# A causal attention kernel with a token sort woven into it: the order of two PSUM readers, of ScalarE's copy, of scatters and loads, and a padded tail

## The chip, the cores and the metric

The kernel runs on one core of one Trainium2 chip. The metric is the device time of one execution in microseconds; lower is better. The runs below fell on three chips, called chip 1, chip 5 and chip 15. A kernel is compared with the kernel before in rounds on the same chip only. Every run here counts as fast but one timed run of the kernel before on chip 15 (881.96 us); the ratios leave it out, the median of 872.19 us has it in. The record does not say on which chip the first comparison ran, nor on which the kernel before was profiled.

## The reference

Attention with a decaying bias is followed by a mixture of experts in which a token goes through one of 8 experts, its own choice or that of the token before it.

```python
batch, n_heads, seq, head_dim = (8, 8, 576, 64)          # experts: 8, D 512, F 1024
scores = q @ k.T / sqrt(64)
cum = cumsum(max(s, 0)); bias = -(cum[i] - cum[j])
scores = where(causal, -1e9, scores + min(bias, 0))
attn = softmax(scores); x = attn @ v                     # -> (8, 576, 512)
logits = x @ w_gate; local_gate = sigmoid(x @ w_local)
for b, s in tokens:                                      # in order of s
    fresh_e = argmax(logits[b, s])
    e = fresh_e if s == 0 or local_gate[b, s] < 0.5 else prev_e
    prev_e = e
    out[b, s] = softmax(logits[b, s])[e] * (relu(x[b, s] @ w1[e]) @ w2[e])
```

## The kernel before

Attention goes through 32 pairs of heads, four pairs to a batch. Scores are held transposed (keys on the partitions), so the sums over keys are TensorE products with a column of ones. 576 is 4 blocks of 128 and a tail of 64. While TensorE makes the scores of pair n, it also finishes pair n - 1: values, sums, and the turning back of x to rows. One iteration:

```python
for n in range(NPAIR + 1):
    b, hp = divmod(n, HP)
    ...                                # loads of q, k, for the next batch
    if b + 1 < B and hp == 1:          # (in the kernel, nested)
        load_v(b + 1, slice(0, HP))    # four transfers of 256 KB at once
    if n + 2 < NPAIR: load_tail(n + 2) # four transfers of 16 KB
    if n: add_up(n - 1)                # VectorE: partial sums of exponentials
    for u, pieces in enumerate((((0, 0), (3, 1)), ((0, 1), (1, 1)), ((2, 0), (2, 1)))):
        scores(n, u)                   # TensorE
        weights(n, *pieces)            # ScalarE: two exponentials a piece; GpSimd: select on the diagonal
    for f in plan.pop((n, 0), ()): f(bank)      # sort work, place 0
    values(n - 1, 0); values(n - 1, 1)          # TensorE; xT copied by VectorE (0) and ScalarE (1)
    weights(n, (1, 0))
    for f in plan.pop((n, 1), ()): f(bank)      # sort work, place 1
    sums(n - 1)      # 36 one-column and 2 two-column products (the trace has two entries for each), then VectorE's reciprocal "recs"
    back(n - 1)      # TensorE: x in rows, VectorE multiplies by recs
    tail(n + 1)
    for f in plan.pop((n, 2), ()): f(bank)      # sort work, place 2
```

The tokens of a group of batches are sorted by expert as soon as its attention is done, in small steps put into the pairs that follow. The groups of batches 0-1, 2-3, 4 and 5 meet their codes in pairs 10, 18, 22 and 26. Their rows go to DRAM by indirect scatters from GpSimd, five to a batch:

```python
for bs in ((0, 1), (2, 3), (4,), (5,)):
    n = HP * bs[-1] + HP + 1
    ...
    at(n + 1, 1, g.fresh, g.share)
    ...
    for i, f in enumerate(g.scatters):
        i = 11 + i // 2 * 2            # two at each second place
        at(n + i // 3, i % 3, f)

def fresh(self, bank):                 # reads the transposed codes in PSUM, 2 x 576
    ...
    nc.scalar.activation(v[:, a:z], x, Act.Relu, bias=...)              # r_v
    nc.vector.tensor_scalar(u[:, a:z], x, 0.0, None, Alu.is_equal)      # r_u

def scatter(self, b, t):
    nc.gpsimd.indirect_dma_start(out=rows_in_dram, out_offset=slots, in_=self.xs[b][:z, t, :], ...)
```

After attention come the experts, about 565 us of dense products.

Of the kernel before, what the change touches and what calls it, by code (L numbers as in the profile page):

```python
# [18 lines left out]
P = 128  # L19
# [44 lines left out]
@with_exitstack  # L64
def kernel(
    ctx: ExitStack,
    tc: tile.TileContext,
    q: bass.AP,
    k: bass.AP,
    vm: bass.AP,  # L70
    vt: bass.AP,
    s: bass.AP,
    w_gate: bass.AP,
    w_local: bass.AP,
    w1: bass.AP,
    w2: bass.AP,
    out: bass.AP,
):
    nc = tc.nc
    mm, tr = nc.tensor.matmul, nc.tensor.transpose  # L80
    cum_d = nc.dram_tensor("cum", (B * H, S), F32, kind="Internal")
    x_d = nc.dram_tensor("x_tokens", (N, D), F32, kind="Internal")
    rows_d = nc.dram_tensor("x_rows", (E * R + 2 * P, XW), F32, kind="Internal")

    ctx.enter_context(tc.manual_schedule(engines=None))
    const = ctx.enter_context(tc.tile_pool(name="const", bufs=1))
    ident = const.tile([P, P], F32, name="ident")
    make_identity(nc, ident)
    lg = const.tile([P, NM, E + 1], F32, name="lg")
    nc.vector.memset(lg, 0.0)  # L90
    recs = const.tile([P, NPAIR, 2 * NB], F32, name="recs")
    nc.vector.memset(recs, 1.0)
    out_of = const.tile([P, 2], I32, name="out_of")
    sort = Sort(tc, const, lg, rows_d, ident)

    with ExitStack() as main:
        keep = main.enter_context(tc.tile_pool(name="keep", bufs=1))
        x4 = keep.tile([P, 4 * NB * XW], F32, name="x4")
        xs = {}

        def new_x(b):
            xs[b] = x4[:, b % 4 * NB * XW : (b % 4 + 1) * NB * XW].rearrange("p (t w) -> p t w", w=XW)
            return xs[b]


        plan = {}

        def at(n, half, *what):
            plan.setdefault((n, half), []).extend(what)

        for bs in ((0, 1), (2, 3), (4,), (5,)):
            n = HP * bs[-1] + HP + 1
            g = sort.group(bs, xs)
            at(n, 1, g.choose)
            at(n, 2, g.codes)
            at(n + 1, 0, g.rows)
            at(n + 1, 1, g.fresh, g.share)
            at(n + 1, 2, g.held)
            at(n + 2, 0, g.hold)
            at(n + 2, 1, g.hot, g.gates)  # L120
            at(n + 3, 0, g.count)
            at(n + 3, 1, g.rank)
            for i, f in enumerate(g.scatters):
                i = 11 + i // 2 * 2
                at(n + i // 3, i % 3, f)
        at(3, 1, sort.constants)
        at(26, 2, sort.early)
        gx = main.enter_context(tc.tile_pool(name="gx", bufs=5))
        w = keep.tile([P, WS], F32, name="w0")
        ready = {"w": {0: w}, "x": {}}  # L130
        for i in range(8):
            at(16 + i // 2, i % 2 * 2, lambda bank, i=i: load_weights(nc, w, w1, w2, EARLY[0], (i,)))

        def fetch_early(bank):
            for i, e in enumerate(EARLY):
                for k in range(2):
                    ready["x"][i, k] = gx.tile([P, XW], F32, name="xg")
                    r0 = e * R + k * P
                    nc.sync.dma_start(ready["x"][i, k], rows_d[r0 : r0 + P, :])

        at(28, 1, fetch_early)

        fx = main.enter_context(tc.tile_pool(name="fx", bufs=2))
        turned = ready["turned"] = Turned(nc, fx, main.enter_context(tc.tile_pool(name="first", bufs=2)), ident)
        for i in range(2):
            at(30 + i, 0, lambda bank, i=i: turned.product(0, i, 2, ready["x"][0, i], bank(1)[0]))
            at(30 + i, 1, lambda bank, i=i: turned.copies(0, i, ready["x"].pop((0, i))))
        last = sort.group((6, 7), xs)

        attention(tc, q, k, vm, vt, s, w_gate, w_local, ident, lg, recs, const, new_x, plan)  # L150
        tables = sort.tables()
        check = in_range(main.enter_context(tc.tile_pool(name="g_sb", bufs=1)), nc, recs, sort.total, sort.ones, out_of)
        hooks = [(2, last.choose), (2, last.codes), (6, last.rows), (6, last.fresh), (6, last.held), (8, last.share),
                 (11, last.hold), (11, last.hot), (13, last.count), (13, last.rank), (15, last.gates),
                 (16, lambda bank: [f(bank) for f in last.scatters]),
                 *((18 + 2 * i, lambda bank: next(tables, None)) for i in range(8)),
                 *((60 + 6 * i, lambda bank, f=f: f(bank)) for i, f in enumerate(check))]
        experts(tc, w1, w2, out, rows_d, ident, sort, early_units() + units(), hooks, x4[:, :WS], gx, ready)
    def number(x, most):
        return nc.values_load(x[0:1, 0:1], min_val=0, max_val=most, skip_runtime_bounds_check_because="a count")  # L160

    ALL = P * NPAIR * 2 * NB
    with tc.If(number(out_of[:, 1:], ALL + MOST[2]) > 0):
        total = number(sort.total, MOST[2])
        with tc.If(total > SLOTS[2]):
            experts(tc, w1, w2, out, rows_d, ident, sort, units(SLOTS[2], SLOTS[2] + 4))
            with tc.If(total > SLOTS[2] + 4):
                experts(tc, w1, w2, out, rows_d, ident, sort, units(SLOTS[2] + 4, MOST[2]))
        with tc.If(number(out_of, ALL) > 0):
            general(tc, q, k, vm, vt, s, w_gate, w_local, w1, w2, out, cum_d, x_d, rows_d, ident, lg)  # L170
# [30 lines left out]


@with_exitstack
def attention(ctx, tc, q, k, vm, vt, s, w_gate, w_local, ident, lg, recs, keep, new_x, plan):



# [39 lines left out]
        nc.sync.dma_start(ins[b][0][:, p], q[b][:, p])  # L247
        other.dma_start(ins[b][1][:, p], k[b][:, p])

    def load_v(b, p, eng=nc.sync):  # L250
        h = slice(2 * p.start, 2 * p.stop)
        for c in range(NF):
            eng.dma_start(vas[b % 2][:, c, h], vm[b][:, c, h])

    def load_tail(n, eng=nc.sync):

        b, hp = divmod(n, HP)
        for h in range(2):
            d = slice(h * DH, h * DH + DH)
            eng.dma_start(kz[d, n % 3, h], k[b][d, hp, TS:])  # L260
            eng.dma_start(vz[d, n % 4, h], vt[b][d, hp])

    tmp = ctx.enter_context(ExitStack())
    t_in = tmp.enter_context(tc.tile_pool(name="t_in", bufs=1))
# [3 lines left out]
    new_batch(0)  # L268

    load_qk(0, first, nc.scalar)  # L270
    kz, vz = (once.tile([P, i, 2, TL], F32, name=name) for name, i in (("kz", 3), ("vz", 4)))
    nc.vector.memset(kz, 0.0)
    nc.vector.memset(vz, 0.0)
    load_tail(0, nc.scalar)
    ones = t_in.tile([BH, S], F32, name="ones")
    nc.vector.memset(ones, 1.0)
# [102 lines left out]
    def tail(n):  # L379

        b, hp = divmod(n, HP)
        for h in range(2):
            mm(banks[1][DH * h : DH * h + DH, :TL], lhsT=kz[:, n % 3, h], rhs=ins[b][0][:, hp, TS:],  # L383
               start=True, stop=True)
        sc = scs[n, "tail"] = p_sc.tile([P, TL], F32, name="tail")
        i = tail_bias + n
        nc.scalar.activation(sc, banks[1][:, :TL], Act.Exp, bias=bias[:, i : i + 1], scale=scale)
# [13 lines left out]
    def values(n, g):  # L401
# [7 lines left out]
                w = piece(n, c, g)  # L409
                some.append((a, z, [(vas[b % 2][:, c, 2 * hp + h, :], w[:, h]) for h in range(2)]))  # L410
        if g == 1:
            some.append((TS, S, [(vz[:, n % 4, h], scs[n, "tail"]) for h in range(2)]))
        for i, (a, z, ops) in enumerate(some):
            for h, (v, w) in enumerate(ops):
                mm(banks[g][DH * h : DH * h + DH, a - q0 : z - q0], lhsT=v, rhs=w,  # L415
# [62 lines left out]
    for n in range(NPAIR + 1):  # L478
        b, hp = divmod(n, HP)
        if b + 1 < B:  # L480
            if hp == 0:
                new_batch(b + 1)
            load_qk(b + 1, slice(hp, hp + 1))
            if hp == 1:
                load_v(b + 1, slice(0, HP))
        if n + 2 < NPAIR:
            load_tail(n + 2)
        if n:
# [1 line left out]
        else:  # L490
            tail(0)
        if n < NPAIR:
            for u, pieces in enumerate((((0, 0), (3, 1)), ((0, 1), (1, 1)), ((2, 0), (2, 1)))):
                scores(n, u)
                weights(n, *pieces)
        for f in plan.pop((n, 0), ()):
# [4 lines left out]
        else:  # L501
            spin(8)
        if n < NPAIR:
            weights(n, (1, 0))
        for f in plan.pop((n, 1), ()):
            f(bank)
        if n:
            sums(n - 1)
            back(n - 1)
        if n + 1 < NPAIR:  # L510
            tail(n + 1)
        for f in plan.pop((n, 2), ()):
# [423 lines left out]
class Group:  # L936
# [51 lines left out]
    def fresh(self, bank):  # L988

        nc = self.s.nc  # L990
        self.u, self.erow = u, v = [self.t(name, [self.nb, S]) for name in "uv"]
        for x, a in zip(self.codes_of, (0, TS)):
            x = x[:, : min(TS, S - a)]
            z = a + x.shape[1]
            nc.scalar.activation(v[:, a:z], x, Act.Relu, bias=self.s.minus[: self.nb])
            nc.vector.tensor_scalar(u[:, a:z], x, 0.0, None, Alu.is_equal)  # L996

    def held(self, bank):

# [349 lines left out]
```

## Time and profile before

| | before |
|---|---|
| time, first runs | 862.7 us, median of 3 (860.55 to 863.55) |
| profiled run | 872.4 us, span 870.7 us |
| pairs 1 to 30 in that run | 275.7 us, of which 242.1 are 30 undisturbed pairs |
| pair 31 and the experts | 580.3 us |

The profiled run took longer than any of the first timed runs. That turned out to matter.

The waits of all engines in the first 340 us of the kernel before are these (engine, line and tile that waited, what it waited for, then us in total, times, and the longest):

```profile
DVE r_u L996 <- ACT r_v L995: 14.6, 5, 3.2
...
PE o L457 <- DVE recs L445: 6.3, 4, 1.8
...
PE o L444 <- issue: 3.9, 8, 0.5
```

A long wait of VectorE costs nothing in itself. It counts because the reciprocal that TensorE needs stands behind it in VectorE's queue: the second line. In the third line TensorE waits for nothing that the profile shows, between its one-column products of the sums (L444). Keep it in mind.

### The profile page before, as it was taken

The numbers are of one execution on the slowest core, as the hardware profiler recorded it, in microseconds if no ns is written. First come the engines' busy times: TensorE is split into PE (matmuls) and PEld (weight loads), VectorE is DVE, ScalarE is ACT, GpSimd is POOL, SyncE is SP. The second block draws the span as 40 slices with busy tenths as digits, with TensorE's granted clock in tenths as the row PEclk, the third lists the DMA queues.
The fourth block names the chain that finished last, engine by engine and source line by source line (L and its number), as shares of the span: only waits on it lengthen the run. The fifth ranks groups of instructions, "written<-read, shape, count | busy, mean of one in ns | idle before, by whom it ended". The sixth has DMA issues, their size and how long they took to land.

```text
span 870.7 us, 20467 instructions
## 1 busy us (share of the span) xinstructions
PE 840.1 (96%) x8319; PEld 602.4 (69%) x8319; DVE 301.2 (35%) x799; ACT 204.2 (23%) x567; POOL 193.1 (22%) x328
## 2 busy tenths in 40 slices
PE   8999999998979999999999999999999999999996
PEld 7777777676758785586567766676667755676662
DVE  4656675765766566301111111111111111111111
ACT  5667566664655410010000000000000000000000
POOL 5423245334534214201100011110011010100001
PEclk9999999998999999999999999999999999999998
DMA  7464266653633508996599666993699934996001
GB/s 212 144 187 139 64 188 229 216 168 111 186 114 114 205 28 283 404 398 211 203 348 394 261 229 214 355 394 143 232 313 376 379 128 169 330 403 249 20 13 40
DMA packets 70359, 191.44 MB, mean 220 GB/s; under 512 B 18061, under 2 KB 19117, under 8 KB 70256
## 3 DMA queue, kind: packets, MB, share of 16 engines
q1 hardware_dynamic: 60896, 159.21, 53.0%
q0 software_dynamic: 8896, 30.47, 9.3%
q8 instruction: 68, 1.11, 0.5%
q10 hardware_dynamic: 464, 0.36, 0.2%
q14 instruction: 35, 0.29, 0.1%
HBM read 166.76 MB, written 23.76 MB: 219 GB/s over the span
## 4 chain that ended last, share of the span: by engine, by line
PE 92%; DVE 3%; ACT 2%; issue 2%; DMA 1%; POOL 0%; POOLq 0%; SPq 0%; ACTq 0%
PE yp L1256 30%; PE hp L1232 27%; PE ps L355 10%; PE o L415 9%; PE o L457 5%; PE hp L1239 4%; PE o L444 3%; ACT sc L364 2%; PE xp L1115 2%; PE o L383 1%; DVE sum L399 1%; DMA kz<-in_k_dram 1%; PE bank L985 0%; DVE sum L396 0%; DVE r_u L996 0%
## 5 line engine op out<-in xcount | busy, mean ns | idle before, releaser
L1256 PE MATMUL yp<-w,hT 128*128 128x512 f32 (+1 forms) x528 | 223.0, 597 | 1.0 <-issue 0.9
L1232 PE MATMUL hp<-xT,w 128*128 128x256 f32 (+1 forms) x1088 | 192.1, 337 | 0.0
L1232 PEld LDWEIGHTS hp<-xT,w 128*128 128x128 f32 x1088 | 172.1, 191 | 23.9 <-issue 8.0
L364 ACT ACTIVATE sc<-ps,bias 128x256 f32<-128x256 f32 (+3 forms) x448 | 157.7, 473 | 34.7 <-PE ps L355 34.5
L1256 PEld LDWEIGHTS yp<-w,hT 128*128 128x128 f32 (+1 forms) x528 | 88.6, 182 | 102.8 <-issue 101.8
L1247 ACT ACTIVATE hT<-hp 128x512 f32<-128x512 f32 x38 | 22.7, 597 | 507.3 <-PE hp L1232 408.9
L1263 POOL DMA_INDIRECT out_dram<-y,at_gate x38 | 38.5, 1012 | 462.5 <-DVE y L1262 447.9
L370 POOL TENSOR_SCALAR_AFFINE_SELECT sc<-sc 128x256 f32<-128x256 f32 x160 | 80.5, 513 | 165.0 <-ACT sc L364 137.1
L1245 DVE TENSOR_SCALAR hT<-hp 128x512 f32<-128x512 f32 x38 | 26.2, 690 | 221.6 <-PE hp L1232 188.4
L355 PE MATMUL ps<-qk 64*128 64x320 f32 (+2 forms) x768 | 96.2, 399 | 0.0
L415 PE MATMUL o<-sc,va 128*64 128x256 f32 (+3 forms) x896 | 90.3, 353 | 0.8 <-DVE tail L393 0.8
L355 PEld LDWEIGHTS ps<-qk 64*128 64x128 f32 x768 | 73.0, 195 | 16.1 <-issue 1.3
L415 PEld LDWEIGHTS o<-sc,va 128*64 128x64 f32 x896 | 56.3, 137 | 28.6 <-issue 4.1
L1262 DVE TENSOR_SCALAR y<-yp,at_gate 128x512 f32<-128x512 f32 x38 | 28.5, 750 | 131.8 <-PE yp L1256 131.8
L1256 PE MATMUL yp<-x,hT 128*128 128x512 f32 (+1 forms) x144 | 65.0, 595 | 0.3 <-issue 0.3
L457 PE MATMUL o<-turn,xT 128*64 128x146 f32 x576 | 49.6, 304 | 7.8 <-DVE recs L445 6.3
L399 DVE TENSOR_TENSOR sum<-sum,sc 128x128 f32<-128x128 f32 (+2 forms) x96 | 53.5, 557 | 3.3
L1123 DVE COPY xT<-xp 128x512 f32<-128x512 f32 x36 | 24.9, 691 | 82.7 <-PE xp L1115 81.3
L1232 PEld LDWEIGHTS hp<-xT,x 128*128 128x128 f32 x320 | 46.1, 191 | 5.8 <-issue 2.6
L1232 PE MATMUL hp<-xT,x 128*128 128x128 f32 (+1 forms) x320 | 50.1, 317 | 0.0
L457 PEld LDWEIGHTS o<-turn,xT 128*64 128x64 f32 x576 | 38.5, 139 | 10.7 <-DVE recs L445 7.7
L461 DVE TENSOR_TENSOR x<-o,recs 128x292 f32<-128x292 f32 x64 | 34.5, 539 | 25.0 <-PE o L457 20.3
(175 smaller groups left out, 574.1 us busy)
## 6 DMA issues: line engine op xcount, KB each, us to landing
w<-in_w_dram SPq DMA_DIRECT2D x184, 512.0 KB
x<-in_w_dram SPq DMA_DIRECT2D x56, 512.0 KB
qk<-in_q_dram SPq DMA_DIRECT2D x32, 288.0 KB
qk<-in_k_dram SPq DMA_DIRECT2D x31, 288.0 KB
xg<-x_rows POOLq DMA_DIRECT2D x30, 293.0 KB
va<-in_vm_dram SPq DMA_DIRECT2D x28, 256.0 KB
x_rows<-r_empty SPq DMA_DIRECT2D x6, 293.0 KB
xg<-x_rows SPq DMA_DIRECT2D x4, 293.0 KB
```

The lines of the kernel that those rows point to most:

```text
L355: mm(ps[:, h, at : at + z - a], lhsT=kb[d, hp, c * P : c * P + P], rhs=qb[d, hp, a:z], start=True, stop=True)
L364: nc.scalar.activation(scs[n, u][:, h, at : at + z - a], raw[u][:, h, at : at + z - a], Act.Exp, bias=bias[:, i : i + 1], scale=scale)
L370: nc.gpsimd.affine_select(out=x, in_=x, compare_op=Alu.is_ge, fill=0.0, base=0, pattern=[[0, 2], [1, P]], channel_multiplier=-1)
L399: add(y, y, piece(n, c, g), op=Alu.add)
L415: mm(banks[g][DH * h : DH * h + DH, a - q0 : z - q0], lhsT=v, rhs=w, start=(i == 0), stop=(i == len(some) - 1))
L457: mm(ps[p : p + TL, t - t0], lhsT=xs["t", g][:, at : at + TL], rhs=w, start=True, stop=True)
L461: nc.vector.tensor_tensor(x, y, rec.unsqueeze(3).to_broadcast([P, t1 - t0, 2, HW]), op=Alu.mult)
L1232: mm(y, lhsT=w[0][:, c, f : f + P], rhs=xT[i][:, c, :], start=(c == 0), stop=(c == DK - 1))
L1239: mm(y[d, m], lhsT=w[h ^ swap][:, c, f + h * HALF : f + h * HALF + HALF], rhs=xT[i][:, c, m], start=(c == 0), stop=(c == DK - 1))
L1256: mm(ps[n * m : n * m + m, :], lhsT=hT[i][:, c, a : a + m], rhs=wn[:, c, :], start=(c == 0), stop=(c == FK - 1))
L1262: nc.vector.tensor_scalar_mul(y, ps, gate[i, k])
L1263: nc.gpsimd.indirect_dma_start(out=next(outs)[:, :], out_offset=bass.IndirectOffsetOnAxis(ap=at[i, k][:, 0:1], axis=0), in_=y[:, :], eleme ...
```

## The change

VectorE reads the codes before ScalarE does, so that its reciprocal comes in time. ScalarE's copy of xT goes ahead of the exponentials of two pieces instead of one (four instructions instead of two). Scatters and loads of v are spread, one to a place or pair instead of two or four at once. The tail's k and v lie padded with zeros in DRAM, so four small transfers a pair become one.

```diff
-                i = 11 + i // 2 * 2
+                i += 11
                 at(n + i // 3, i % 3, f)
...
-    def load_v(b, p, eng=nc.sync):
+    def load_v(b, p, cs=range(NF), eng=nc.sync):
         h = slice(2 * p.start, 2 * p.stop)
-        for c in range(NF):
+        for c in cs:
             eng.dma_start(vas[b % 2][:, c, h], vm[b][:, c, h])
...
-        b, hp = divmod(n, HP)
-        for h in range(2):
-            d = slice(h * DH, h * DH + DH)
-            eng.dma_start(kz[d, n % 3, h], k[b][d, hp, TS:])
-            eng.dma_start(vz[d, n % 4, h], vt[b][d, hp])
+        eng.dma_start(kvz[:, n % 4], kvt[n])
...
-    nc.vector.memset(kz, 0.0)
-    nc.vector.memset(vz, 0.0)
...
-            if hp == 1:
-                load_v(b + 1, slice(0, HP))
...
-            for u, pieces in enumerate((((0, 0), (3, 1)), ((0, 1), (1, 1)), ((2, 0), (2, 1)))):
+            for u, pieces in enumerate((((0, 0), (3, 1)), ((0, 1), (1, 1)), ((2, 0),))):
...
-            weights(n, (1, 0))
+            weights(n, (2, 1), (1, 0))
...
+        if b + 1 < B:
+            load_v(b + 1, slice(0, HP), (hp,))
...
+            nc.vector.tensor_scalar(u[:, a:z], x, 0.0, None, Alu.is_equal)
             nc.scalar.activation(v[:, a:z], x, Act.Relu, bias=self.s.minus[: self.nb])
-            nc.vector.tensor_scalar(u[:, a:z], x, 0.0, None, Alu.is_equal)
```

The padded array `kvt` is built from the inputs where they are laid out for the kernel.

More of the change, by code (lines that the diff above doesn't have):

```diff
@@ L71 @@
     vt: bass.AP,
+    kvt: bass.AP,
     s: bass.AP,
@@ L148 @@
         last = sort.group((6, 7), xs)
-        attention(tc, q, k, vm, vt, s, w_gate, w_local, ident, lg, recs, const, new_x, plan)
+        attention(tc, q, k, vm, kvt, s, w_gate, w_local, ident, lg, recs, const, new_x, plan)
         tables = sort.tables()
@@ L203, in attention @@
 @with_exitstack
-def attention(ctx, tc, q, k, vm, vt, s, w_gate, w_local, ident, lg, recs, keep, new_x, plan):
+def attention(ctx, tc, q, k, vm, kvt, s, w_gate, w_local, ident, lg, recs, keep, new_x, plan):
     nc = tc.nc
@@ L270, in attention @@
     load_qk(0, first, nc.scalar)
-    kz, vz = (once.tile([P, i, 2, TL], F32, name=name) for name, i in (("kz", 3), ("vz", 4)))
-    nc.vector.memset(kz, 0.0)
-    nc.vector.memset(vz, 0.0)
+    kvz = once.tile([P, 4, 2, 2, TL], F32, name="kvz")
     load_tail(0, nc.scalar)
@@ L382, in tail @@
         for h in range(2):
-            mm(banks[1][DH * h : DH * h + DH, :TL], lhsT=kz[:, n % 3, h], rhs=ins[b][0][:, hp, TS:],
+            mm(banks[1][DH * h : DH * h + DH, :TL], lhsT=kvz[:, n % 4, 0, h], rhs=ins[b][0][:, hp, TS:],
                start=True, stop=True)
@@ L411, in values @@
         if g == 1:
-            some.append((TS, S, [(vz[:, n % 4, h], scs[n, "tail"]) for h in range(2)]))
+            some.append((TS, S, [(kvz[:, n % 4, 1, h], scs[n, "tail"]) for h in range(2)]))
         for i, (a, z, ops) in enumerate(some):
@@ L1326, in pairs @@
         return a.reshape(B, HP, 2, S, DH).transpose(0, 2, 4, 1, 3).reshape(B, P, HP, S)
-    v = i["v"]
+    k, v = i["k"], i["v"]
+    kvt = _np.zeros((NPAIR, 2, TL, 2, 2, TL), _np.float32)
+    for h in range(2):
+        kvt[:, h, :, 0, h] = k[:, h::2, TS:].reshape(NPAIR, TL, DH).transpose(0, 2, 1)
+        kvt[:, h, :, 1, h] = v[:, h::2, TS:].reshape(NPAIR, TL, DH)
     arrays = {
@@ L1333 @@
         "vt": v[:, :, TS:].reshape(B, HP, 2, TL, DH).transpose(0, 2, 3, 1, 4).reshape(B, P, HP, DH),
+        "kvt": kvt.reshape(NPAIR, P, 2, 2, TL),
         "s": i["s"].reshape(B * H, S),
```

## The prediction

> **What bounds the kernel now.** I read the busy line of the page first, then busy time by stretches of time, then the waits and the timeline of single pairs.
>
> ```profile
> PE 840.1 (96%) x8319; PEld 602.4 (69%) x8319; DVE 301.2 (35%) x799; ACT 204.2 (23%) x567; POOL 193.1 (22%) x328
> ```
>
> TensorE is the bound: only time in which it idles, works at a lower clock, or does extra work can be won. The change touches attention (about 9 to 305 us) and one line of the sort that also runs once among the experts. So I cut attention into stretches (columns: window, its length, then busy us of PE, PEld, DVE, ACT, POOL, then the granted clock, DMA share, GB/s):
>
> ```profile
> 9.00:90.00 81.00, 80.37 (x1452) 63.72 (x1453) 47.67 (x112) 55.61 (x163) 28.96 (x64) 1.00 0.58 169
> 90.00:109.00 19.00, 17.21 (x306) 13.17 (x302) 11.82 (x30) 10.72 (x32) 5.85 (x14) 0.91 0.20 55
> 158.00:180.00 22.00, 20.21 (x336) 15.57 (x334) 14.35 (x38) 12.05 (x35) 6.12 (x15) 0.92 0.53 172
> 197.00:223.00 26.00, 22.14 (x332) 17.30 (x332) 14.25 (x39) 12.04 (x35) 12.68 (x18) 0.87 0.36 116
> 239.00:272.00 33.00, 28.02 (x478) 21.71 (x476) 20.16 (x60) 17.22 (x50) 9.05 (x21) 0.95 0.41 122
> ```
>
> Up to 90 us TensorE is full at clock 1.00; then come four stretches with idle time and a lower clock. They are the pairs in which the sort of a group of batches runs. From the starts of the score matmuls an undisturbed pair takes 8.07 us. Pairs 1 to 30 took 290.36 - 14.67 = 275.7 us, against 30 x 8.07 = 242.1: an excess of 33.6. It divides into TensorE's own sort work (four groups of about 1.7 us, two turned blocks of 0.6, so 8.0), idle time (nine windows that cover 9 to 305 us: 296.0 less 279.3 busy, so 16.7) and clock: (1 - clock) x length of the four windows above is 1.7 + 1.8 + 3.4 + 1.7 = 8.6. The sum is 33.3, so nothing large is missing.
>
> Next, one such pair, the eleventh (n = 10), on three engines (start, duration, engine and instruction, then in brackets the idle before it and its releaser):
>
> ```profile
> 95.56 0.86 ACT L995 ACTIVATE r_v<-bank,r_minus 2x512 f32<-2x512 f32 x2
> ...
> 96.25 0.81 DVE L996 TENSOR_SCALAR r_u<-bank 2x512 f32<-2x512 f32 x2 [2.91 <-ACT r_v L995]
> ...
> 97.58 0.16 DVE L445 RECIPROCAL recs<-o 128x10 f32<-128x10 f32 x1
> ...
> 97.79 1.53 PE L457 MATMUL o<-turn,xT 128*64 128x146 f32 x12 [1.78 <-DVE recs L445]
> ...
> 99.46 3.83 PE L355 MATMUL ps<-qk 64*128 64x320 f32 x24
> ```
>
> VectorE stands 2.91 us because it reads the codes in PSUM after ScalarE does, and ScalarE comes to them only after its copy of xT (94.67) and two exponentials. The reciprocal of the sums queues behind, and TensorE waits 1.78 us for it. The granted clock around that wait:
>
> ```profile
> 96.00:97.80 1.80, 0.02 (x3) 0.01 (x2) 1.42 (x6) 0.42 (x2) 0.15 (x1) 1.00 0.14 31
> 97.80:99.50 1.70, 1.70 (x18) 1.58 (x18) 0.60 (x2) 0.00 (x0) 0.00 (x0) 0.57 0.00 0
> 99.50:101.00 1.50, 1.50 (x8) 1.11 (x8) 1.50 (x2) 0.31 (x1) 0.00 (x0) 0.50 0.00 0
> 101.00:103.30 2.30, 2.30 (x21) 1.76 (x19) 2.23 (x6) 1.65 (x5) 0.42 (x2) 0.90 0.00 0
> ```
>
> Each stall is paid twice: 1.8 us of waiting, then 0.43 x 1.7 + 0.50 x 1.5 + 0.10 x 2.3 = 1.7 us at the lower clock.
>
> **What the skill says.** "PSUM — Partial Sum Buffer", section "PSUM bank collisions raise a hardware error", says that two engines may not access one bank in the same partitions at once, two reads included. So the order between the two readers cannot be dropped, only turned; the trace agrees, with the first read of VectorE at 96.25, after ScalarE's at 95.56. "TensorE: Matmul & The Clock Gate", section "HAM oscillation — how this bites in real kernels", puts the harm at idle gaps above some 3.4 us; here a gap of 1.8 us was enough for 0.50, so the trace is harsher and decides. "DMA: Bandwidth & Descriptors", section "Specifications", asks for at least 512 B a transfer; the page has 18,061 packets under 512 B, the tails among them, but TensorE waited only 0.2 us in all of attention for such a load, at the start.
>
> **The change part by part.**
>
> *Codes read by VectorE first.* No instruction is added. The order listing of both kernels shows the two reads of r_u losing their wait for ScalarE, and ScalarE's r_v gaining one for VectorE; the scan that needs both comes after the next multiply. In pair 10 the codes are in PSUM at 91.7, VectorE is free at 93.3 after its copy, so r_u (0.81) and the three small den steps (0.6) end near 94.8, before TensorE's sums are done (95.4). The stall should vanish. Pairs 10 and 11 together took 3.32 + 1.39 us above 8.07, of which 0.67 + 0.37 is sort work: 3.67 to win. Pairs 18 and 19: 2.66 + 2.05 less 1.04, again 3.67. Pair 22 has the same wait, hidden in the profile under a row of short stalls of matmul issue with nothing waited for (204.8 to 210.2 us); I book 3.5. Pair 26: a wait of 1.21 with 0.48 of issue before it; I book 1.7 and, as pair 27 has a late reciprocal of its own, only 0.3 of clock. Sum 3.67 + 3.67 + 3.5 + 2.0 = 12.8 us.
>
> *ScalarE's copy ahead of four exponentials.* The same count of exponentials; two of 256 columns (about 0.4 us each) move behind the copy. In a clean pair the copy waits for TensorE anyway (0.44 us), so nothing is won there. It counts where ScalarE begins late: its first exponential starts 1.24 us into a clean pair but 2.27, 2.50 and 2.85 in pairs 14, 15 and 21, and there TensorE waited 0.20, 0.44 and 0.79 for the copy. Sum 1.4 us. The price: the last selects of a pair come some 0.9 us later, at about 88.3 for those due when VectorE adds at 89.3 and TensorE uses them at 91.6. It fits with a small margin.
>
> *Scatters spread.* Each costs GpSimd about 1.0 us (1,026 ns mean in attention). Pairs with two scatters around their start are those where ScalarE begins late. Alternate halves get one each now, but two halves with no select between them still issue back to back, so only part is cured. TensorE waited 1.6 + 0.3 + 0.3 us for PSUM banks that ScalarE freed late; I take 0.7.
>
> *Loads of v spread.* TensorE never waited for v, so the four 256 KB loads moving over four pairs win nothing on the path: 0.
>
> *Tail padded.* Four transfers of 16 KB become one of 128 KB, 1 KB a partition; the two memsets (0.38 + 0.48) go. At the start the chain is: memsets, then the tail's DMA from 4.24 to 9.33, then the tail matmul at 9.37. The new load need not wait for memsets and is issued near 1.4 us; the bias transposes end at 8.9, which then bound. Gain 0.5 us. Later tails are hidden either way.
>
> Sum: 12.8 + 1.4 + 0.7 + 0 + 0.5 = 15.4 us, so 862.7 - 15.4 = 847.3. I predict 847.
>
> **Rivals.**
>
> First, *a wait takes the place of the one removed*. ScalarE now reads the codes after four exponentials, so r_v ends near 97.8 in pair 10, about when the next tail exponential is due, and VectorE's scan waits for it; and two scatters after a later last select can push the next pair's selects and ScalarE's start. Against it: ScalarE idles 1.2 us or more twice in nearly every such pair. For it: VectorE is busy 11.8 of 19 us there. If each of the four pairs keeps 1 us and its clock loss, half of the 12.8 stays: 854.
>
> Second, *the row of issue stalls in pair 22 is a real cost that spreading cures*. It is 5.3 us in the profiled run, with the loads of v and the scatters near. But the DMA engines moved nothing for much of it, and the profiled run took 872.4 against 862.7 timed, so I hold it for mostly a thing of the profiled run. If it is real and goes: 842.
>
> Third, *the gain is hidden by the experts*, if their weights or sort tables came no earlier. Against it: those loads start after attention releases its buffers, so they shift along. If it held, half would go: 855.
>
> **Range and chances.** The first part carries four fifths of the sum and is well shown for pairs 10 and 18, less for 22 and 26. Rival one or three would add up to 8 us, rival two take off 5. So 840 to 855 holds it 8 times in 10. Faster by over 2% needs under 845.4, a gain of 17.3, a little more than my sum: 0.35. Within 2%: 0.64. Slower: 0.01, since nothing is added to TensorE.
>
> **What would show it.** Right: VectorE's idle before r_u (14.6 us in 5) nearly gone; TensorE's wait for recs (6.3 us in 4) under 2, for ScalarE's copy (1.4 us) near 0; pairs 10, 11, 18, 19 at about 8.7, 8.4, 8.7, 8.4; clock above 0.97 in the windows that had 0.91 and 0.92; first scores near 9.2 instead of 9.63; clean pairs still 8.07; the experts' length unchanged. Wrong: the same wait under another name (the scan behind r_v, sums behind a late select, banks behind ScalarE), or an experts part that is longer by what attention won.

## The result, and the profile after

| | before | after |
|---|---|---|
| time | 861.62 us, median of 4 (859.17 to 863.55) | 849.59 us, median of 4 (848.11 to 853.0) |
| ratio after/before | | 0.9867, 95% interval 0.9825 to 0.991 |
| span of the profiled run | 870.7 us | 846.9 us |
| first scores | 9.63 us | 8.99 us |
| pairs 1 to 30 | 275.7 us | 252.2 us |
| pair 31 and the experts | 580.3 us | 580.6 us |

Ratios are the mean time of one kernel's fast runs over that of the other's of the same rounds, so they are not quite the ratio of the medians quoted. By the 2% rule the verdict is the same time, with a small real gain.

The page after shows TensorE's busy time 11.3 us lower with the same 8,319 entries, a granted clock of nine tenths or more in every slice, and a chain of waits that is nearly all TensorE:

```profile
PE 828.8 (98%) x8319; PEld 595.6 (70%) x8319; DVE 300.2 (35%) x797; ACT 204.0 (24%) x567; POOL 198.7 (23%) x328
...
PEclk9999999999999999999999999999999999999999
...
PE 97%; DVE 1%; issue 1%; POOL 0%; POOLq 0%; SPq 0%
```

Two of the stretches that had the stalls, in the columns of the prediction, are now full and at clock 1.00:

```profile
90.00:109.00 19.00, 18.98 (x336) 14.76 (x336) 14.27 (x34) 13.28 (x40) 7.61 (x17) 1.00 0.19 61
...
157.00:180.00 23.00, 22.99 (x451) 18.30 (x452) 16.99 (x46) 14.84 (x45) 7.84 (x18) 1.00 0.51 163
```

Of the waits shown of before, one is left in attention, in pair 27:

```profile
PE o L452 <- DVE recs L440: 1.1, 1, 1.1
```

(L452 and L440 are L457 and L445 of before.) Pair 10 in the timeline of the changed kernel:

```profile
92.38 0.80 DVE L990 TENSOR_SCALAR r_u<-bank 2x512 f32<-2x512 f32 x2
...
94.41 1.46 PE L452 MATMUL o<-turn,xT 128*64 128x146 f32 x18
...
94.52 0.22 DVE L440 RECIPROCAL recs<-o 128x10 f32<-128x10 f32 x1 [0.74 <-PE o L439]
...
95.36 0.86 ACT L991 ACTIVATE r_v<-bank,r_minus 2x512 f32<-2x512 f32 x2
...
96.00 0.81 PE L350 MATMUL ps<-qk 64*128 64x320 f32 x4
```

VectorE reads the codes without a wait, and now the reciprocal waits for TensorE, not TensorE for it. The 18 entries of L452 run in one go. (The last line is cut off by its window: a pair has 24 products of scores.) The profiled spans differ by 23.8 us: 0.64 at the start, 23.49 in pairs 1 to 30, and -0.29 after them. But the timed difference is 12.0 us. So the profiled run of before holds some 12 us of loss that its timed runs of the first comparison did not have. The experiments had to find out what that loss is as well.

### The profile page after: what moved, and what is told of

Same layout as the page of the kernel before. It is cut to its first block, busy times and chain, and to the rows that moved or that the text cites. A ratio compares the mean times of both kernels' runs of the same rounds, so it can differ in the third digit from the quotient of the medians.

```text
span 846.9 us, 20276 instructions
## 1 busy us (share of the span) xinstructions
PE 828.8 (98%) x8319; PEld 595.6 (70%) x8319; DVE 300.2 (35%) x797; ACT 204.0 (24%) x567; POOL 198.7 (23%) x328
## 2 busy tenths in 40 slices
DMA packets 64725, 193.50 MB, mean 228 GB/s; under 512 B 8333, under 2 KB 13485, under 8 KB 64624
## 4 chain that ended last, share of the span: by engine, by line
PE 97%; DVE 1%; issue 1%; POOL 0%; POOLq 0%; SPq 0%
PE yp L1251 31%; PE hp L1227 28%; PE ps L350 10%; PE o L410 10%; PE o L452 5%; PE hp L1234 4%; PE o L439 3%; PE xp L1110 2%; PE o L304 1%; PE o L378 1%; PE bank L980 0%; DVE sum L394 0%; DVE sum L391 0%; PE o L434 0%; PE bank L1024 0%
## 5 line engine op out<-in xcount | busy, mean ns | idle before, releaser
L365 POOL TENSOR_SCALAR_AFFINE_SELECT sc<-sc 128x256 f32<-128x256 f32 x160 | 84.3, 540 | 137.1 <-ACT sc L359 130.0
L350 PE MATMUL ps<-qk 64*128 64x320 f32 (+2 forms) x768 | 91.5, 385 | 0.0
L350 PEld LDWEIGHTS ps<-qk 64*128 64x128 f32 x768 | 69.6, 187 | 14.7
L452 PE MATMUL o<-turn,xT 128*64 128x146 f32 x576 | 47.2, 296 | 1.4 <-DVE recs L440 1.1
L1069 POOL DMA_INDIRECT x_rows<-x,r_slot_i x40 | 41.4, 1036 | 10.1 <-issue 7.3
```

The costliest lines, as they stand in the source:

```text
L350: mm(ps[:, h, at : at + z - a], lhsT=kb[d, hp, c * P : c * P + P], rhs=qb[d, hp, a:z], start=True, stop=True)
L365: nc.gpsimd.affine_select(out=x, in_=x, compare_op=Alu.is_ge, fill=0.0, base=0, pattern=[[0, 2], [1, P]], channel_multiplier=-1)
L452: mm(ps[p : p + TL, t - t0], lhsT=xs["t", g][:, at : at + TL], rhs=w, start=True, stop=True)
L1069: self.s.nc.gpsimd.indirect_dma_start(out=next(self.s.views)[:, :], out_offset=bass.IndirectOffsetOnAxis(ap=self.slot[:z, m : m + 1], axis=0),
```

## The experiments

All kernels gave correct results. Times are medians; the last column is the length of pairs 1 to 30 in that kernel's profiled run.

| run | what it is | chip | time (before beside it) | ratio, 95% | pairs 1-30 |
|---|---|---|---|---|---|
| codes_only | only the order of the readers | 1 | 850.60 (860.59) | 0.9875, 0.9843-0.9907 | 253.5 |
| no_codes | all but that order | 1 | 863.23 (860.59) | 1.0016, 0.9985-1.0047 | 268.2 |
| copy_only | only ScalarE's copy moved | 1 | 866.32 (860.59) | 1.0048, 1.0011-1.0085 | 271.4 |
| tail_only | only the padded tail | 1 | 860.45 (860.59) | 0.9982, 0.9947-1.0017 | 262.1 |
| after_again | the changed kernel | 5 | 851.10 (871.64) | 0.9752, 0.9708-0.9796 | 252.6 |
| no_copy | all but the copy | 5 | 888.08 (871.64) | 1.0193, 1.0141-1.0246 | 295.2 |
| copy_fill | copy_only, its stalls filled | 5 | 871.66 (871.64) | 1.0003, 0.9957-1.0049 | 271.2 |
| early27 | all, one sort step a pair later | 5 | 850.65 (871.64) | 0.9747, 0.9704-0.9791 | 253.6 |
| no_copy_h2 | no_copy, other places for scatters | 15 | 863.75 (872.19) | 0.9909, 0.9872-0.9945 | 264.7 |
| no_copy_b | no_copy again | 15 | 890.46 (872.19) | 1.0238, 1.0198-1.0278 | 291.6 |
| codes_b | codes_only again | 15 | 864.35 (872.19) | 0.9923, 0.9897-0.9950 | 271.5 |
| no_scat | all but the spread scatters | 15 | 855.06 (872.19) | 0.9810, 0.9779-0.9841 | 255.6 |

The theory at the start: nearly all of the gain is the wait for the codes and the clock lost after it. The rivals: the spread scatters or the copy carry the gain, and a new wait takes the place of the old.

### First set, chip 1: one part alone, or all but one

**codes_only** is the kernel before with two lines changed round:

```diff
+            nc.vector.tensor_scalar(u[:, a:z], x, 0.0, None, Alu.is_equal)
             nc.scalar.activation(v[:, a:z], x, Act.Relu, bias=self.s.minus[: self.nb])
-            nc.vector.tensor_scalar(u[:, a:z], x, 0.0, None, Alu.is_equal)
```

> Only VectorE's read of the codes goes ahead of ScalarE's. Theory (the wait for recs carries the gain): the four stalls of some 1.8 us and the lower clock after them go; VectorE's idle before r_u falls from 14.6 us to under 3, TensorE's wait for recs from 6.3 to under 2.5; of the 12 us that the whole change won in timed runs, 8 to 11 come from here (851 to 854 beside a before of 862). Rival (the late starts of ScalarE beside the scatters, and the transfers, carry it): 1 to 4 us, 858 to 861.

It gave 0.9875 against the changed kernel's 0.9867 in the first comparison. Where the kernel before takes 860 us, two lines are the whole gain within the error.

**no_codes** is the changed kernel with those two lines put back.

```diff
             nc.scalar.activation(v[:, a:z], x, Act.Relu, bias=self.s.minus[: self.nb])
+            nc.vector.tensor_scalar(u[:, a:z], x, 0.0, None, Alu.is_equal)
```

(The same line above the activation is removed.)

> The whole change less its first part: ScalarE still reads the codes before VectorE, and now after four exponentials. Theory: only 1 to 4 us are won, 858 to 861; and since r_v comes two exponentials later, VectorE's idle before r_u is longer than before (about 3.7 us a time against 2.9) and TensorE's wait for recs longer too, so it may even be slower than before. Rival: 8 us or more are won, 854 or less.

Nothing is left of the gain: 1.0016, where 1 to 4 us had been expected to stay or even less. VectorE waited 17.1 us for ScalarE's r_v, 5 times, and TensorE 9.8 us for the reciprocals, more than the 14.6 and 6.3 us of before.

**copy_only** says why those waits grew:

```diff
-            ... ((0, 1), (1, 1)), ((2, 0), (2, 1)))):
+            ... ((0, 1), (1, 1)), ((2, 0),))):
...
-            weights(n, (1, 0))
+            weights(n, (2, 1), (1, 0))
```

> Only ScalarE's copy goes ahead of the exponentials. Theory: its wait before TensorE (1.4 us) goes, but r_v comes 0.8 us later behind two more exponentials, four times, so that TensorE's wait for recs grows by about 3 us: 0 to 3 us slower than before (862 to 865). Rival (ScalarE's late copies carry the gain): 3 us or more faster.

The copy alone makes the kernel slower, by 0.5% (interval 0.1 to 0.9). Its waits in the first 340 us:

```profile
DVE r_u L996 <- ACT r_v L995: 17.2, 5, 3.6
...
PE o L457 <- DVE recs L445: 10.1, 5, 2.5
```

ScalarE comes to the codes after four exponentials now instead of two. With ScalarE first, that delays VectorE and so TensorE. With VectorE first it delays only the scan, which has slack. So the two parts are not independent: the copy move is harmful before the order is turned and harmless after it.

**tail_only** takes the tail's part of the diff alone (the two memsets go too).

```diff
-        for h in range(2):
-            d = slice(h * DH, h * DH + DH)
-            eng.dma_start(kz[d, n % 3, h], k[b][d, hp, TS:])
-            eng.dma_start(vz[d, n % 4, h], vt[b][d, hp])
+        eng.dma_start(kvz[:, n % 4], kvt[n])
```

> Only the padded tail, one transfer a pair. Theory: the first scores start 0.5 us earlier (about 9.1 instead of 9.63) and nothing else moves: 0 to 1.5 us faster. Rival (8,192 fewer small packets relieve what else waits on transfers): 3 us or more faster.

No effect that these runs can show: 0.9982, interval 0.9947 to 1.0017. Its first scores came at 10.03 us in its profile, later than before's 9.63. In the fourteen profiles the first scores lie anywhere from 8.77 to 10.16 us, with the new tail from 8.77 to 10.16 too, so the 0.5 us booked at the start can't be told from that scatter.

tail_only has the stalls of before, and shows something about the clock. Pair 10 took 10.70 us and pair 11 only 8.51, the length without any clock loss; pair 18 took 10.70 and pair 19 10.12, with it. In the 1.5 to 2 us from the start of pairs 11, 19, 23 and 27 the granted clock was 1.00, 0.60, 1.00 and 0.72. In copy_only, where the waits are about 2.5 us, it was 0.50 in all four. So a stall of this size (TensorE stood 1.76, 1.75, 1.63 and 1.63 us) costs the clock in some cases and not in others.

The clock records of the traces show in what portions it is paid. In every trace the granted clock changes only at moments that lie a whole number of 3.41 us apart. In the attention of before it is at 0.50 for 3.41, 3.41, 6.83 and 3.41 us, in tail_only for 3.41 us twice, in copy_only for 6.83, 6.83, 3.41 and 6.83 us. One portion costs about half its length, 1.7 us (an estimate from these numbers), which is what the prediction worked out for pair 10. What decides whether a stall brings one, two or none is not shown.

### Is the clock loss the stall's own?

**copy_fill** is copy_only with 18 products of no use put into the stall of pairs 10, 18, 22 and 26, so that TensorE does not idle while it waits for the reciprocal.

```diff
+            if t0 == 3 and n + 1 in (10, 18, 22, 26):
+                for _ in range(18):
+                    mm(banks[1][:, 3 * P :], lhsT=ident, rhs=ident, start=True, stop=True)
```

> Only the copy moved, as in the run before (866 us), plus 18 matmuls of the identity into an unused corner of a PSUM bank where TensorE stands for the reciprocal in pairs 10, 18, 22 and 26; about 2.3 us of work that nobody reads, where 2.5 us of standing were. Theory (each stall is paid twice, once as waiting and once as lower clock): the wait stays, as filler, but the clock stays at 1.00 after it, and 6 to 10 us are won against the kernel with the copy alone (856 to 860). Rival (the low clock afterwards does not bound anything, or comes from something else than the idle time): no gain, 865 to 869, or slower by the added work.

The granted clock after the wait in pair 10, in copy_only (windows; the column before the last two is the clock):

```profile
97.95:99.80 1.85, 1.85 (x16) 1.72 (x16) 0.54 (x2) 0.00 (x0) 0.00 (x0) 0.50 0.00 0
99.80:101.50 1.70, 1.70 (x10) 1.29 (x10) 1.70 (x2) 0.31 (x1) 0.00 (x0) 0.50 0.00 0
```

and in copy_fill, from its first scores of pair 11 on:

```profile
100.35:103.30 2.95, 2.95 (x30) 2.26 (x26) 2.91 (x6) 2.02 (x6) 0.50 (x2) 1.00 0.00 0
```

The clock stays at 1.00, and pairs 11, 19 and 23 take 8.51, 8.51 and 8.50 us instead of 10.42, 10.22 and 9.40. So the second half of the stall's price is the idling itself, and it goes away when TensorE is kept busy. The fill is no remedy: it lasts longer than the stall, so pairs 10 and 18 take 13.1 us instead of 12.3, and the time equals before's (1.0003). The 6 to 10 us expected against the copy alone, 856 to 860 us, did not come. What the copy alone takes on chip 5 was not measured, so the fill's worth in time stays open; the clock is what this run shows.

### Second set, chip 5: the same kernels, another picture

**after_again** is the changed kernel, unaltered, sent along as a reference for the set.

```diff
(no edit against the changed kernel)
```

> The changed kernel once more, beside the others of this set on one chip. Both theories: about 849 to 851, 1.1 to 1.4% faster than before; it is the yardstick for the kernel without the copy's move and for the one with the early rows moved.

The kernel before took 871.64 us here, 11 us more than on chip 1. The changed kernel took 851.1, close to its 849.59 of the first comparison. So the gain is 2.5% here (1.1 to 1.4% was expected) and 1.3% in the first comparison, and what varies is the kernel before.

**no_copy** is the changed kernel with the copy in its old place.

```diff
-            ... ((0, 1), (1, 1)), ((2, 0),))):
+            ... ((0, 1), (1, 1)), ((2, 0), (2, 1)))):
...
-            weights(n, (2, 1), (1, 0))
+            weights(n, (1, 0))
```

> The whole change less the copy's move (codes first, scatters, loads of v and tail stay). Theory (with the codes first nobody waits for the copy or for r_v): within 1.5 us of the changed kernel, and ScalarE's wait for the copy costs TensorE under 0.5 us. Rival (my prediction's second part, 1.4 us): 1.4 us or more slower than the changed kernel, with TensorE's wait for ScalarE's xT over 1 us.

That was a plain miss: 888.08 us, 37 us slower than the changed kernel and 1.9% slower than before (by the 2% rule that verdict is unclear). **no_copy_b** is the same kernel on chip 15, to see whether this was that chip's alone.

```diff
(no edit against no_copy)
```

> The kernel without the copy's move once more, as reference for the one before on the same chip. Where before takes 872: 885 to 892. Where before takes 860 (a chip that hardly minds scatters over sums): theory says that it is then only 0 to 5 us slower than the changed kernel, 850 to 856; rival (the copy's place itself): again some 37 us slower.

It gave 890.46 us, as expected for a chip where before takes 872. The timeline of pair 13 in no_copy_b (TensorE's sums L439, GpSimd's scatters L1069, VectorE's reciprocal L440; in brackets the idle time before an entry):

```profile
118.69 0.31 PE L439 MATMUL o<-one,sc 128*32 128x1 f32 x16
...
119.09 1.02 POOL L1069 DMA_INDIRECT x_rows<-x,r_slot_i  x1 [0.16 <-issue]
...
120.41 0.32 PE L439 MATMUL o<-one,sum 128*32 128x1 f32 x12 [0.48 <-issue]
...
121.35 0.23 PE L439 MATMUL o<-one,sum 128*32 128x1 f32 x3 [0.48 <-issue]
...
122.01 0.97 POOL L1069 DMA_INDIRECT x_rows<-x,r_slot_i  x1 [0.30 <-issue]
...
123.77 0.22 DVE L440 RECIPROCAL recs<-o 128x10 f32<-128x10 f32 x1 [5.43 <-PE o L452]
```

and of the same pair in the changed kernel:

```profile
117.91 1.13 POOL L1069 DMA_INDIRECT x_rows<-x,r_slot_i  x1 [0.17 <-issue]
...
118.91 0.31 PE L439 MATMUL o<-one,sc 128*32 128x1 f32 x16
...
119.84 0.22 DVE L440 RECIPROCAL recs<-o 128x10 f32<-128x10 f32 x1 [1.29 <-PE o L439]
```

In the changed kernel the scatter starts a microsecond ahead of the sums, which take 0.9 us, and the reciprocal follows at once. In no_copy_b three scatters (the one at 120.72 is left out above) lie over and just behind the sums. The one-column products come in small lots with half a microsecond between them and nothing waited for, the sums take 2.9 us, and the reciprocal comes 2.2 us after the last of them, 0.8 us after the last scatter ended. Over all pairs of no_copy_b, all eight sums that took longer than 1.3 us had 0.7 us or more of scatters over them (the shortest 1.7 us with 0.7, the longest 4.2 us with 2.9).

The copy's place sets this because of GpSimd's order. In no_copy GpSimd makes all four selects of a pair before the scatter of place 0, and the fourth waits for ScalarE's later exponentials; so the scatter comes 6.05 us into pair 13, and the sums 5.65. In the changed kernel the fourth select belongs behind the copy, the scatter goes ahead of it, at 4.66 us, and the sums start at 5.66.

**no_copy_h2** tests the position. It keeps the copy where it was and changes only the places of the scatters, to two at each end of a pair:

```diff
-                i += 11
+                i = 11 + i // 2 * 3
```

> The kernel without the copy's move (888 us beside a before of 872 on its chip), with the same 30 scatters put two at a time at the end of a pair, so that none is issued before TensorE's sums. Theory (a scatter that GpSimd works on while TensorE does its one-column sums holds up TensorE, VectorE and ScalarE for some us, on some chips): no scatter over the sums, pairs 13 to 16 fall from 9 to 14 us to under 9, and the time to within 6 us of the changed kernel's, 849 to 857. Rival (scatters cost what they cost, wherever they are; or the copy's place itself made the 37 us): 875 or more on a chip like that. On a chip where before takes 860, both kernels would be near 850 and the run would not tell them apart.

It took 863.75 us against 890.46 of no_copy_b on the same chip, with the same instructions: 26.7 us from the position of 30 scatters alone. No sums overlap a scatter in its profile, and all take about 0.9 us. But it missed the expected 849 to 857 us, and one pair tells why:

```profile
217.47 0.91 POOL L1069 DMA_INDIRECT x_rows<-x,r_slot_i  x1 [0.30 <-issue]
223.49 0.17 DVE L1043 CAST r_slot_i<-r_slot 128x5 int32<-128x5 f32 x1 [8.91 <-DMA x_rows<-x,r_slot_i]
...
223.92 1.00 PE L452 MATMUL o<-turn,xT 128*64 128x146 f32 x6 [8.01 <-DVE recs L440]
```

The next group's slots go into a tile that the last group's scatters still read, because my places put those late. VectorE waits 8.9 us, TensorE 8.0. That pair is 9.0 us longer than in the changed kernel, out of 12.5 us for pairs 1 to 30 together. (The third line is cut off by its window.) It is a new wait that this experiment brought in, not a sign against the theory. In the same profile the part from pair 31 on is longer too, 588.1 us against 580.6 and 583.1 in the two profiles of the changed kernel; that part is not explained.

**early27** tries to mend the wait that is left in the changed kernel, in pair 27, the pair in which VectorE has the most to do.

```diff
-        at(26, 2, sort.early)
+        at(27, 2, sort.early)
```

> The changed kernel with the counts for the early rows taken one pair later, out of VectorE's fullest pair (27, 1.5 us over its neighbours). Theory: pair 27 falls from 10.06 to about 8.6 us and pair 28 rises by at most 0.3: 0.5 to 1.5 us faster than the changed kernel, if the later fills do not hold up the early fetch. Rival: the fetch of the early rows comes too late and the experts start later: 1 us or more slower.

Pair 27 fell to 8.51 us, but pairs 28 to 30 took 9.15, 9.20 and 9.49 us instead of about 8.7, 8.1 and 8.7. The time is the same: 850.65 against 851.10; the 0.5 to 1.5 us expected do not show. The work moved and took its wait along.

### Third set, chip 15: the parts where before is slow

**codes_b** is codes_only on such a chip.

```diff
(no edit against codes_only)
```

> Codes first alone, once more. Where before takes 860: 850, as measured. Where before takes 872: theory says that codes first takes away the stalls of recs there too, but leaves the three or four scatters that meet sums or ScalarE's start, so it keeps part of the extra 10: 853 to 861, and the whole change is worth more than this part there. Rival: 848 to 852, codes first is all of it everywhere.

It won 7.8 us only by the medians (0.77% by the ratio, which leaves out the slow run of before: about 6.7 us), of the 20.5 us by which the changed kernel wins on chip 5, and missed the expected 853 to 861 us. The profiles of the same kernel on the two chips can be laid side by side in pair 22. On chip 1 (codes_only), the scatter is L1074, the sums L444, the reciprocal L445:

```profile
195.42 0.90 POOL L1074 DMA_INDIRECT x_rows<-x,r_slot_i  x1 [0.28 <-issue]
...
195.60 0.31 PE L444 MATMUL o<-one,sc 128*32 128x1 f32 x16
...
197.60 0.22 DVE L445 RECIPROCAL recs<-o 128x10 f32<-128x10 f32 x1 [1.88 <-PE o L457]
```

and on chip 15 (codes_b):

```profile
204.02 0.90 POOL L1074 DMA_INDIRECT x_rows<-x,r_slot_i  x1 [0.28 <-issue]
...
204.20 0.31 PE L444 MATMUL o<-one,sc 128*32 128x1 f32 x16
...
208.55 0.28 PE L444 MATMUL o<-one,sum 128*32 128x1 f32 x4 [1.21 <-issue]
...
210.65 0.22 DVE L445 RECIPROCAL recs<-o 128x10 f32<-128x10 f32 x1 [6.32 <-PE o L444]
```

In both, the sums begin 0.18 us after a scatter does. On chip 1 they are done in 1.0 us, and only the reciprocal is late, by 0.64 us of TensorE's time. On chip 15 they trickle for 6.4 us while four scatters run. The profiled run of before has the same row in its pair 22: sums of 6.0 us, 3.7 of them under scatters. So that run looks like one of chips 5 and 15, and what differs there is how hard scatters over the sums hit. Other pairs agree: with 0.98 and 0.99 us of scatters over them the sums of pair 14 took 1.17 us in copy_only (chip 1) and 2.36 us in copy_fill (chip 5), and with 0.73 and 0.77 us those of pair 26 took 0.98 us in tail_only (chip 1) and 1.76 us in codes_b. Each chip was used in one set only, so the chip itself and the occasion are not told apart.

**no_scat** is the changed kernel with the scatters two at a time again.

```diff
-                i += 11
+                i = 11 + i // 2 * 2
```

> The whole change less the spreading of the scatters. Theory: with the copy's move the second-half pairs of scatters start after the late select, past the sums, so only the pairs of scatters of the first half (15 and 22) can meet sums: within 3 us of the changed kernel where before takes 860, 0 to 6 us slower than it where before takes 872. Rival (spreading is what cures the scatters): 8 us or more slower than the changed kernel where before takes 872.

It took 855.06 us. That is 9.3 us less than codes_b, for the copy, the loads of v and the tail together, and by ratios (0.9810 and 0.9752, on two chips of like times) some 0.6% or 5 us more than the changed kernel. The changed kernel did not run on chip 15 and the two intervals overlap, so these 5 us are not clear of noise. Two sums are still hit, in pairs 14 and 22 (2.1 and 1.8 us), which take 10.48 and 9.70 us instead of 8.07 and 8.81. Spreading takes the scatters off the sums, but only with the copy moved: no_copy_b, which has the spreading without it, took 26 us more than codes_b.

## Why the prediction was right, and where it was right by luck

It said 847 us and 840 to 855; 849.59 was measured. The mechanism of its main step is shown, and the signs it named came true but one: no wait of VectorE for ScalarE's read is left in attention, TensorE's wait for the reciprocal fell from 6.3 to 1.1 us, that for ScalarE's copy from 1.4 to 0, pairs 10, 11, 18 and 19 take 8.81, 8.51, 8.82 and 8.51 us (about 8.7 and 8.4 were predicted), clean pairs still 8.07. The exception is the first scores near 9.2 us: they came at 8.99, but tail_only shows that this can't be put down to the tail. Its terms fared less evenly. (A small slip in its sum: of the 16.7 us of idle time 1.2 lie outside pairs 1 to 30, where 275.69 less 260.23 busy leaves 15.5; so 1.6 us of the excess are left over and not 0.3.)

**Codes first, 12.8 us booked.** The pairs booked against what codes-first alone did in the profiles. On chip 1, tail_only stands for the kernel before, as the tail changed nothing that could be told; for the slower chips, the profiled run of before stands against codes_b:

| pairs | booked | chip 1 (tail_only to codes_only) | slower chips (before to codes_b) |
|---|---|---|---|
| 10, 11 | 3.67 | 19.21 - 17.32 = 1.89 | 20.85 - 17.32 = 3.53 |
| 18, 19 | 3.67 | 20.82 - 17.33 = 3.49 | 20.85 - 17.33 = 3.52 |
| 22, 23 | 3.5 | 19.16 - 18.19 = 0.97 | 24.72 - 25.63 = -0.91 |
| 26, 27 | 2.0 | 20.83 - 18.40 = 2.43 | 23.11 - 19.31 = 3.80 |
| all of 1 to 30 | 12.84 | 262.05 - 253.46 = 8.59 | 275.69 - 271.50 = 4.19 |

Pairs 18 and 19 are within 0.2 us of the booking in both. The term that was mis-sized is pair 22: "I book 3.5" was an assumption behind the row of issue stalls, and turning the readers round did not touch that row. On chip 1 there is no such row: there TensorE's wait for the reciprocal in pair 22 fell from 1.63 to 0.64 us, and no clock had been lost after it. Also on chip 1, pairs 10 and 11 gained less, since there the clock had not been lost after the 1.8 us stall. On the slower chip most of the rest was given back in pairs 14 and 15 (16.92 us before, 23.52 in codes_b), where the scatters now came to lie over the sums. Timed, the part is worth 10.0 us on chip 1 and about 7 on chip 15.

**The copy, 1.4 us, and the scatters, 0.7.** Both were sized as single waits taken off the path, and this is the step that failed. On a chip like chip 1 they are worth nothing that shows (ratio 0.9867 for the whole change, 0.9875 for the readers' order alone), beyond 0.5% lost by the copy alone. On the slower chips, with codes first, the copy, the loads of v and the tail together give 9.3 us and the spreading some 5 more (not clear of noise), while the spreading without the copy (with the tail and the loads, no_copy_b against codes_b) costs 26 us. Their worth is in where the scatters fall against TensorE's sums. The prediction looked at what a scatter delays on GpSimd and ScalarE, and not at what runs on TensorE meanwhile.

**The loads of v, 0, and the tail, 0.5.** The tail fits in both size and doubt. Packets under 512 B fell from 18,061 to 8,333 with no time won, as predicted. The loads of v were not run alone, so their 0 is not shown; they went along with parts that give nothing on chip 1.

**The rivals.** The first, that a wait takes the place of the one removed, did not come true in the whole change: only 0.8 us of the scan's wait for r_v is left, off the path. A part of the change does make a wait longer: with ScalarE first, the moved copy lengthens VectorE's from 14.6 to 17.2 us. The second, that the row of stalls in pair 22 is real and is cured by spreading, was right in its first half where it was given up. "I hold it for mostly a thing of the profiled run" fails, and so does a reading behind it, "the DMA engines moved nothing for much of it": from 204.80 to 210.20 us they moved 1.02 MB, 189 GB/s on average with gaps between, and 0.97 MB of it went through the software queue, on which that stretch has only the four scatters. The same row stands in codes_b's profile on chip 15, pair 22 fell from 15.69 us to 8.81, and where the kernel before takes 872 us the gain is 2.5%, not 1.3. But spreading is not the main cure: pair 22 took 16.81 us in codes_b, 9.70 in no_scat, which has the copy's move (with the loads and the tail) but not the spreading, and 8.81 with both. The third fell: from pair 31 on it is 580.3 us before and 580.6 after (583.1 in after_again).

So the gain booked, 15.4 us, fits neither kind of chip: 12.0 us were measured in the first comparison and 20.5 on chip 5. The sizes were read from a profiled run of 872 us and taken off a time of 862.7 us, which the prediction noticed and used against rival two alone. In the first comparison too much was booked for the readers' order (10.0 us on chip 1), the copy, the scatters and the tail; on the other chips again too much for the readers' order (about 7 us), and too little for the copy and the scatters. The time lies in the range for either kind, since the changed kernel takes about 850 us in both comparisons; the prediction gave no reason for that, and that part was luck.

**What stays open.** Why a scatter holds up one-column products and the semaphores between TensorE and VectorE, and why it does so on chips 5 and 15 far more than on chip 1. Shown is only that the same instructions at other places cost 26.7 us less, and that the same kernel with the same alignment took 1.0 us on one chip and 6.4 on another. Whether it is the chip, or something else that differed between the three sets, is not shown either. It is also open whether the changed kernel would keep its evenness if its scatters fell otherwise. No version beat it: early27 only ties.

## What to carry to other kernels

Where two engines must read one PSUM tile in turn, let the one read first that stands nearer to TensorE's next wait. Before a short wait of TensorE is dismissed, add the slower clock after it. Where indirect scatters run beside a row of one-column products, look in the timeline at where each scatter falls, on more than one chip, and judge a reordering by that as well: parts of such a change do not add up.

## What the Trainium skill lacked or had wrong

- "TensorE: Matmul & The Clock Gate", section "HAM oscillation — how this bites in real kernels", puts the harm at idle gaps above about 3.4 us. Here gaps of 2.5 us brought a granted clock of 0.50 every time (copy_only, four of four), and gaps of 1.6 to 1.8 us lowered it in two cases of four (tail_only: 0.60 and 0.72 against 1.00 and 1.00). Section "What's actually happening" gives a window of about 3.4 us and calls it free-running. The traces agree on the length: the clock changes only at whole multiples of 3.41 us (low for 3.41, 3.41, 6.83 and 3.41 us in the attention of before). How busy TensorE must be within a window is not shown by the runs.
- "DMA: Bandwidth & Descriptors", section "SWDGE vs HWDGE vs iDMA", tells of VectorE in its 2-port mode locking GpSimd out of the memory that it writes descriptors to. I found nothing there on TensorE's products being held up while GpSimd scatters, as seen here: one-column products under scatters took 2.9 us (no_copy_b) and 6.4 us (codes_b) instead of 0.9, and a reciprocal of VectorE came 2.2 us after its input was done, 0.8 us after the last scatter (no_copy_b).
- None of the pages that I read says that chips differ at this: the kernel before took 860.59 us on chip 1 and 871.64 and 872.19 us on chips 5 and 15 (all runs but one in the fast state, one set on each chip), and the changed kernel about 850 in both comparisons.
- "DMA: Bandwidth & Descriptors", section "Specifications", asks for at least 512 B a transfer. It could add that this is worth nothing where transfers are hidden: 9,728 fewer packets under 512 B won no time that shows (tail_only, 0.9982, 0.9947 to 1.0017).
